# Retention attention and a routed MLP on one core: score blocks computed in 64x64 quadrants instead of 128x128 blocks

## The chip, the cores and the metric

The kernel runs on one core of a Trainium2 chip. The metric is the device time of one execution in microseconds (us). Matrix products run on TensorE (PE; its weight loads are listed apart as PEld), elementwise work on VectorE (DVE) and ScalarE (ACT). The queues of SyncE (SP), ACT and GpSimd (POOL) issue the transfers.

## The reference

Only this much of it matters here. For each of 8 batches and 8 heads, with 576 tokens and 64 features per head:

```python
scores = scale * np.matmul(q, k.transpose(0, 1, 3, 2))
gamma = 1.0 - 2.0 ** (-5.0 - np.arange(H))
Dmat = np.where(rel >= 0, gamma ** rel, 0.0)       # rel = query position - key position
ret = scores * Dmat
attn = np.matmul(ret, v)
```

The result is laid out as 4608 tokens by 512 features and goes through a gate (8 experts, each token to one expert with room for 576) and the chosen expert's two matrix products with a ReLU between them. Everything is in float32. What bears on the change: a score counts only where the key is not later than the query.

## The kernel before, in words

The attention stage goes through 16 units `u`; a unit is a pair of heads in a pair of batches, so four sequences of 576 tokens. Each sequence is cut into four chunks of 128 tokens and a tail of 64. The 64 features of two heads fill the 128 partitions of a `q` or `k` tile (partitions 0 to 63 and 64 to 127, `half(0)` and `half(1)`), and the two batches lie side by side.

The powers of gamma are split off: the values `v` are scaled by ScalarE (`vscale`), the output by a table `ex` when it leaves the accumulator (`evict`). So inside a 128-token chunk only the causal mask remains. Per half unit `hf` (two chunks, two batches: four blocks of 128 keys by 128 queries for each of two heads) the steps are:

- `A(u, hf)`, line 566: the scores of the chunks with themselves, keys on the output's partitions, queries on its columns, into the accumulator tile `pA` (two banks, one buffer). Line 568: VectorE multiplies `pA` by the mask `m1` and writes `am`.
- `A2(u)`, line 577: the tail's scores, in 64x64 pieces; masked into `amt`.
- `across`, line 601: earlier chunks' running state `S` times the queries, into `pX` (one buffer). The pieces are 64 by 64 with 128 query columns (64 for the tail).
- `ST`, line 589: the update of the state, evicted by ScalarE (line 591).
- `within`, line 610: `am` times the values, added in `pX`. `within2`, line 617: the same for the tail.
- `evict`, line 630: VectorE scales `pX` into the tile `xT`.
- "fills": pieces of the gate (lines 643, 656, 658), of row transposes and stores (lines 667, 675), and of the routing (lines 151 to 233), hung at fixed places between the units.

`A` is called half a unit ahead: the order on TensorE is A of the next half, (A2), across, ST, within, ST, (within2, across of the tail), fills. Each engine executes its queue in the order in which the program is written; nothing is reordered by the kernel. The loads of unit `u + 2` are issued on SP at the start of unit `u` into three rotating buffers, so they wait until unit `u - 1` has been read.

After the last unit the routing search, then eight experts' products follow; that part is not touched.

Of the kernel before, what the change touches and what calls it, by code (L numbers as in the profile page):

```python
# [10 lines left out]
F32 = mybir.dt.float32  # L11
# [3 lines left out]
ALU = mybir.AluOpType  # L15
# [3 lines left out]
B, H, S, D = 8, 8, 576, 64  # L19
NP, HP, NB = 4, 4, 9  # L20
N, DM, E, FF = 4608, 512, 8, 1024
SLACK = 1.0

CST = HP * 18 + 128 + 64

def consts_np():
    h = np.arange(H); g = (1.0 - 2.0 ** (-5.0 - h)).astype(np.float64)
    p = np.arange(128)
    at = np.where(np.arange(NB) < 8, 128 * (np.arange(NB) // 2), 512)[None] + np.where(np.arange(NB) < 8, p[:, None], p[:, None] % 64)
    vs = g.reshape(HP, 1, 2)[None] ** -at[:, None, :, None].astype(np.float64)  # L30
    m1 = p[:, None] <= p[None, :]
    m2 = p[:, None] % 64 <= np.arange(64)[None, :]
    ex = 0.125 * g.reshape(HP, 2)[:, p // 64].T[:, :, None] ** np.arange(S)
    f = lambda a: np.ascontiguousarray(a, dtype=np.float32).reshape(128, -1)
    return np.concatenate([f(vs), f(m1), f(m2), f(ex)], axis=1)

def layout(q, k, v):

    def pairs(a):
        a = a.reshape(NP, 2, HP, 2, S, D).transpose(0, 2, 3, 1, 4, 5)  # L40
        m = a[..., :512, :].reshape(NP, HP, 2, 2, 4, 128, D).transpose(0, 1, 2, 4, 3, 5, 6).reshape(NP, HP, 2, 1024, D)
        t = a[..., 512:, :].reshape(NP, HP, 2, 128, D)
        return np.concatenate([m, t], axis=3)
    second = np.concatenate([np.arange(1024) // 128 % 2, np.arange(128) // 64])[None, None, None, :, None] == 1
    cross = lambda a: np.where(second, a[:, :, ::-1], a)
    T = lambda a: cross(pairs(a)).transpose(0, 1, 2, 4, 3).reshape(NP, HP, 128, 1152)
    N = lambda a: a.reshape(NP, HP, 2, NB, 128, D).transpose(0, 1, 4, 3, 2, 5)
    vn = N(pairs(v)).copy()
    vn[:, :, :, 8, 1] = np.roll(vn[:, :, :, 8, 1], 64, axis=2)
    qk = np.ascontiguousarray(np.stack([T(q), T(k)], axis=2))  # L50
    vk = np.ascontiguousarray(np.concatenate([vn.reshape(NP, HP, 128, NB * 128), N(pairs(k)).reshape(NP, HP, 128, NB * 128)[..., :1024]], axis=3))
    return qk, vk
# [445 lines left out]
def attention(tc, nc, P, qk, vk, cst_d, wg_d, rf, xd, Lg):  # L498
    cst = P['c'].tile([128, CST + HP*S], F32, name="cst", tag="xg")
    vs = cst[:, 0:HP*18].rearrange("p (h q) -> p h q", h=HP)  # L500
    m1, m2 = cst[:, CST-192:CST-64], cst[:, CST-64:CST]
    ex = cst[:, CST:].rearrange("p (h q) -> p h q", h=HP)
    wg = P['a'].tile([128, HP, 32], F32, name="wg")
    LD = {}
# [16 lines left out]
    def consts(hp):  # L521
        part(CST + S*hp, CST + S*hp + S)
    load(0, "kqvn", (512,))
    load(1, "kqvn", (512,))

    def fetch(order):
        for x in order.split():
            if x == "c":
                part(0, CST)
            elif x[0] == "h":  # L530
# [6 lines left out]
    PS, AM, PX, XT = {}, {}, {}, {}  # L537
    ident = P['ident']
    SI = {}
    half = lambda x: slice(64*x, 64*x + 64)  # L540
# [7 lines left out]
            nc.scalar.activation(x, x, AF.Copy, scale=vs[:, u % HP, 4*c+h:4*c+h+1])  # L548

    two = P['open']("pa")  # L550
    PS2 = P['ps'].tile([128, 4, 64], F32, name="pS", tag="r", bufs=1)

    def A(u, hf):

        if u == 16: return
        if hf == 0 and 2 <= u + 1 < 16:
            if u < 3:
                consts(u + 1)
            if u == 2:
                R.fetch(nc, rf)  # L560
                nc.sync.dma_start(wg[:, :, 0:8], wg_d.rearrange("(hp p) e -> p hp e", p=128))
        pa = two.tile([128, 2, 4, 128], F32, name="pA", tag="A", bufs=1)
        for j in range(4):
            s = slice(512*hf + 128*j, 512*hf + 128*j + 128)
            for r in range(2):
                nc.tensor.matmul(pa[:, r, j], LD[u, 'k'][half(r), s], LD[u, 'q'][half(r), s], start=True, stop=True, skip_group_check=True)  # L566
        AM[u, hf] = P['w'].tile([128, 2, 4, 128], F32, name="am", bufs=2)
        nc.vector.tensor_tensor(AM[u, hf], pa, m1[:, None, None, :].to_broadcast([128, 2, 4, 128]), op=ALU.mult)  # L568

    def A2(u):  # L570

# [9 lines left out]
    def ST(u, c):  # L581

        if u == 16: return
        if c == 0: PS[u] = PS2[:, 2*(u % 2):2*(u % 2)+2]
        v, n = LD[u, 'v'], LD[u, 'n']
# [165 lines left out]
    vscale(0, 1)  # L751
    P['warm'](7)
    A(0, 0)
    ST(0, 0)
    nc.gpsimd.memset(wg, 0.0)
# [58 lines left out]
    c = R.first_digits(30, 36)  # L814
# [245 lines left out]
def build(tc, nc, qk, vk, cst, wg, rf, w1, w2, out):  # L1060
    with ExitStack() as top:
# [4 lines left out]
        top.enter_context(tc.manual_schedule())  # L1066
        xd = dr.tile([N, DM], F32, name="xd")
        full = P['c'].tile([128, 512], BF16, name="full")
# [66 lines left out]
```

## Time and profile before

| what | value |
|---|---|
| time, median of 3 runs | 650.63 us (650.55 to 651.21) |
| the profiled execution | 651.56 us, span 649.8 us |
| PE busy over the span | 610.9 us (94%) |
| VectorE busy over the span | 406.5 us (63%) |
| transfers of 576 KB of keys, issue to landing, median | 7.2 us |
| last masking of scores (line 568) starts | 136.8 us |

The attention stage fills the first 143 us or so of the span, the routing and the experts the rest. Busy shares count an engine as busy from the start of an instruction to its end; several matrix products can be under way at once, so a sum of their durations says less than the distance between their starts.

### The profile page before, as it was taken

The numbers are of one execution on the slowest core, as the hardware profiler recorded it, in microseconds if no ns is written. First come the engines' busy times: TensorE is split into PE (matmuls) and PEld (weight loads), VectorE is DVE, ScalarE is ACT, GpSimd is POOL, SyncE is SP. The second block draws the span as 40 slices with busy tenths as digits, with TensorE's granted clock in tenths as the row PEclk, the third lists the DMA queues.
The fourth block names the chain that finished last, engine by engine and source line by source line (L and its number), as shares of the span: only waits on it lengthen the run. The fifth ranks groups of instructions, "written<-read, shape, count | busy, mean of one in ns | idle before, by whom it ended". The sixth has DMA issues, their size and how long they took to land.

```text
span 649.8 us, 14770 instructions
## 1 busy us (share of the span) xinstructions
PE 610.9 (94%) x5756; PEld 519.3 (80%) x5756; DVE 406.5 (63%) x1504; ACT 288.8 (44%) x584; POOL 140.9 (22%) x189
## 2 busy tenths in 40 slices
PE   8899898978969998999999999988999999999995
PEld 5687777756569878977987898788779889989984
DVE  3567979778747887987996897777783302301300
ACT  4455555523265236552563356144615724643500
POOL 0000000000311072162153142241314234131111
PEclk9999999989979999999999999998999999999998
DMA  9998999743497469889599199747966995893521
GB/s 333 400 391 281 348 350 351 266 98 131 155 215 176 140 173 246 212 193 263 110 245 261 59 223 227 208 106 172 201 188 146 227 264 141 174 269 117 98 66 40
DMA packets 51704, 134.20 MB, mean 207 GB/s; under 512 B 5810, under 2 KB 19762, under 8 KB 51634
## 3 DMA queue, kind: packets, MB, share of 16 engines
q0 software_dynamic: 14960, 51.91, 36.7%
q1 hardware_dynamic: 36530, 81.08, 36.0%
q8 instruction: 45, 0.74, 0.5%
q10 hardware_dynamic: 144, 0.26, 0.1%
q14 instruction: 25, 0.20, 0.1%
HBM read 81.33 MB, written 18.87 MB: 154 GB/s over the span
## 4 chain that ended last, share of the span: by engine, by line
PE 68%; DVE 15%; DMA 6%; issue 6%; POOL 2%; ACT 2%; SPq 0%; POOLq 0%; DVEq 0%; ACTq 0%
PE ph L963 25%; PE py L1002 24%; PE pA L566 4%; PE pX L610 3%; DMA qin<-in_qk 2%; PE pS L589 2%; PE pX L601 2%; PE r L332 2%; PE pt L934 2%; DMA w1l<-raw 1%; PE pT L643 1%; DVE am L568 1%; DVE xT L630 1%; POOL xg L919 1%; DMA cst<-in_cst 1%
## 5 line engine op out<-in xcount | busy, mean ns | idle before, releaser
L1002 PE MATMUL py<-w2h,hb 128*128 128x512 f32 x576 | 188.2, 399 | 0.0
L963 PE MATMUL ph<-xh,w1h 128*128 128x320 f32 (+1 forms) x512 | 153.7, 304 | 2.7 <-ACT xh L936 1.5
L963 PE MATMUL ph<-xh,w1l 128*128 128x320 f32 (+1 forms) x512 | 151.3, 299 | 4.6 <-DMA w1l<-raw 4.2
L963 PE MATMUL ph<-xl,w1h 128*128 128x320 f32 (+1 forms) x512 | 151.0, 299 | 0.2 <-issue 0.2
L1002 PE MATMUL py<-w2l,hb 128*128 128x512 f32 (+1 forms) x320 | 125.1, 391 | 0.0
L1002 PEld LDWEIGHTS py<-w2h,hb 128*128 128x128 f32 x576 | 104.0, 188 | 20.6
L963 PEld LDWEIGHTS ph<-xh,w1l 128*128 128x128 f32 x512 | 97.7, 192 | 5.4 <-DMA w1l<-raw 4.4
L967 ACT ACTIVATE hb<-ph 128x256 fp32r<-128x256 f32 (+1 forms) x128 | 51.7, 410 | 112.5 <-PE ph L963 103.9
L963 PEld LDWEIGHTS ph<-xh,w1h 128*128 128x128 f32 x512 | 97.8, 192 | 4.7 <-ACT xh L936 1.9
L963 PEld LDWEIGHTS ph<-xl,w1h 128*128 128x128 f32 x512 | 97.9, 192 | 0.7 <-DVE cs L336 0.3
L970 DVE SCALAR_TENSOR_TENSOR hb<-ph,hb 128x256 fp32r<-128x256 f32 (+1 forms) x192 | 59.0, 352 | 60.2 <-ACT hb L967 56.6
L919 POOL DMA_INDIRECT xg<-xd,idx x40 | 40.8, 1020 | 202.1 <-DMA raw<-in_w 168.8
L1002 PEld LDWEIGHTS py<-w2l,hb 128*128 128x128 f32 (+1 forms) x320 | 56.7, 177 | 12.7
L979 POOL DMA_INDIRECT out_y<-yt,idx x40 | 40.9, 1022 | 118.4 <-ACT yt L1019 76.4
L1019 ACT ACTIVATE yt<-py 128x512 f32<-128x512 f32 x32 | 19.2, 598 | 105.3 <-PE py L1002 79.8
L908 POOL DMA_DIRECT2D w2l<-raw x32 | 28.8, 900 | 126.5 <-ACT hb L967 117.8
L548 ACT ACTIVATE vin<-vin,cst 128x128 f32<-128x128 f32 (+1 forms) x160 | 48.2, 379 | 6.8 <-DMA vin<-in_vk 6.8
L568 DVE TENSOR_TENSOR am<-pA,cst 128x1024 f32<-128x1024 f32 x32 | 39.1, 1221 | 18.0 <-PE pA L566 17.7
L1022 DVE TENSOR_TENSOR yt<-yt,py 64x512 f32<-64x512 f32 x8 | 5.4, 679 | 69.5 <-ACT yt L1021 69.3
L566 PEld LDWEIGHTS pA<-qin,kin 64*128 64x128 f32 x512 | 32.1, 191 | 16.1 <-DVE am L568 7.8
L566 PE MATMUL pA<-qin,kin 64*128 64x128 f32 x512 | 38.3, 289 | 6.9 <-DVE am L568 5.0
L591 ACT ACTIVATE S<-pS 128x128 f32<-128x128 f32 x64 | 17.6, 276 | 51.1 <-PE pS L589 51.1
(177 smaller groups left out, 877.4 us busy)
## 6 DMA issues: line engine op xcount, KB each, us to landing
raw<-in_w SPq DMA_DIRECT2D x64, 512.0 KB, 5.5
w2l<-raw POOLq DMA_DIRECT2D x32, 512.0 KB
w1l<-raw POOLq DMA_DIRECT2D x31, 512.0 KB
kin<-in_qk SPq DMA_DIRECT2D x14, 576.0 KB, 7.2
qin<-in_qk SPq DMA_DIRECT2D x14, 576.0 KB
vin<-in_vk SPq DMA_DIRECT2D x14, 576.0 KB, 7.2
nin<-in_vk SPq DMA_DIRECT2D x14, 512.0 KB, 10.5
xd<-xr SPq DMA_DIRECT2D x36, 192.0 KB, 4.0
```

What stands on the lines that cost most here:

```text
L548: nc.scalar.activation(x, x, AF.Copy, scale=vs[:, u % HP, 4*c+h:4*c+h+1])
L566: nc.tensor.matmul(pa[:, r, j], LD[u, 'k'][half(r), s], LD[u, 'q'][half(r), s], start=True, stop=True, skip_group_check=True)
L568: nc.vector.tensor_tensor(AM[u, hf], pa, m1[:, None, None, :].to_broadcast([128, 2, 4, 128]), op=ALU.mult)
L610: nc.tensor.matmul(PX[u, hf][half(h), b, 128*c:128*c+128], v[:, a:a+64], AM[u, hf][:, h ^ b, j], start=False, stop=False, skip_group_check ...
L908: nc.gpsimd.dma_start(lo, raw, accum_op=ALU.add)
L919: nc.gpsimd.indirect_dma_start(out=xg[:n, j, :], out_offset=None, in_=xd[:, :], in_offset=bass.IndirectOffsetOnAxis(ap=found[e][:n, j:j+1] ...
L963: T.matmul(ps, w, x, start=(k == 0), stop=(k == 11))
L967: A.activation(hb[:, f, c], ps, AF.Relu)
L970: V.scalar_tensor_tensor(hb[:, f, to+a:to+b], ps[:, a:b], 0.0, hb[:, f, 256*s+a:256*s+b].bitcast(F32), op0=ALU.max, op1=ALU.subtract)
L979: st = nc.gpsimd.indirect_dma_start(out=out[:, :], out_offset=bass.IndirectOffsetOnAxis(ap=found[e][:n, t:t+1], axis=0), in_=y[:n], in_off ...
L1002: T.matmul(ps[:m], a, w, start=(k == 0), stop=(k == last), skip_group_check=True)
L1019: A.activation(y, ps, AF.Copy)
```

## The change

The block of 128 keys by 128 queries is cut at key 64. The first 64 keys meet all 128 queries; the last 64 keys meet only the last 64 queries, since the mask leaves nothing of the first 64. Each piece is a product of its own with 64 keys on the output's partitions, so a block that was one product of 128 by 128 is now one of 64 by 128 and one of 64 by 64.

In every second chunk the keys (with their copies of `k` by row and their `v`) are turned by 64 tokens on the host, so that there the long piece lies on the other half of the output's partitions. The mask for these chunks is turned too: `m1` becomes a tile of two masks, copied twice side by side by VectorE at the start, and the constants grow by 128 columns (64 KB). `pA` becomes one tile for the whole stage, set to zero once at the start; the quarter that is never written stays zero, and the mask multiplies it by zero.

```diff
-    m1 = p[:, None] <= p[None, :]
+    m1 = np.stack([turned(c)[:, None] <= p[None, :] for c in range(2)], axis=1)
...
     two = P['open']("pa")
+    pa = two.tile([128, 2, 4, 128], F32, name="pA", tag="A", bufs=1)
+    nc.vector.memset(pa, 0.0)
+    nc.vector.tensor_copy(m1, cst[:, CST-320:CST-64].rearrange("p (c q) -> p c q", c=2)[:, :, None, :].to_broadcast([128, 2, 2, 128]))
...
-        pa = two.tile([128, 2, 4, 128], F32, name="pA", tag="A", bufs=1)
-        for j in range(4):
-            s = slice(512*hf + 128*j, 512*hf + 128*j + 128)
-            for r in range(2):
-                nc.tensor.matmul(pa[:, r, j], LD[u, 'k'][half(r), s], LD[u, 'q'][half(r), s], start=True, stop=True, skip_group_check=True)
+        k, q = LD[u, 'k'], LD[u, 'q']
+        for j in (0, 2, 1, 3):
+            s = 512*hf + 128*j
+            for t in (j//2, 1 - j//2):
+                x = 64*(t ^ j//2)
+                for r in range(2):
+                    nc.tensor.matmul(pa[half(t), r, j, x:], k[half(r), s+x:s+x+64], q[half(r), s+x:s+128], start=True, stop=True, skip_group_check=True)
         AM[u, hf] = P['w'].tile([128, 2, 4, 128], F32, name="am", bufs=2)
-        nc.vector.tensor_tensor(AM[u, hf], pa, m1[:, None, None, :].to_broadcast([128, 2, 4, 128]), op=ALU.mult)
+        nc.vector.tensor_tensor(AM[u, hf], pa, m1.rearrange("p c b q -> p (c b) q")[:, None].to_broadcast([128, 2, 4, 128]), op=ALU.mult)
```

On TensorE one half unit reads, before (unit 1's second step; a row is a run of equal products, with the output's shape):

```order
L566 MATMUL pA_212<-qin_92,kin_91 128x128 x8
L601 MATMUL pX_223<-qin_88,S_190 64x128 x4
L601 MATMUL pX_223<-qin_88,S_204 64x128 x4
L589 MATMUL pS_117<-vin_89,nin_90 64x64 x4
L610 MATMUL pX_223<-am_172,vin_89 64x128 x8
```

and in the changed kernel, where the same lines are 577, 612, 600 and 621:

```order
L577 MATMUL pA_118<-qin_93,kin_92 64x128 x2
L577 MATMUL pA_118<-qin_93,kin_92 64x64 x2
...
L577 MATMUL pA_118<-qin_93,kin_92 64x128 x2
L577 MATMUL pA_118<-qin_93,kin_92 64x64 x2
L612 MATMUL pX_248<-qin_89,S_208 64x128 x4
L612 MATMUL pX_248<-qin_89,S_222 64x128 x4
L600 MATMUL pS_121<-vin_90,nin_91 64x64 x4
L621 MATMUL pX_248<-am_190,vin_90 64x128 x8
```

Nothing changed places; the eight products of the block became sixteen (the pair of rows four times), and the other steps stand as they stood.

On VectorE the program begins, before, so (with the semaphores that a row waits for):

```order
L1069 MEMSET full_66 128x512
L1073 TENSOR_SCALAR ident_70<-it_68 128x128 [waits Pool_49]
L568 TENSOR_TENSOR am_139<-pA_130,cst_85 128x1024 [waits DMAHW2_49,PE_49]
```

and in the changed kernel so:

```order
L1080 MEMSET full_66 128x512
L1084 TENSOR_SCALAR ident_70<-it_68 128x128 [waits Pool_49]
L558 MEMSET pA_118 128x1024
L559 COPY m1_86<-cst_85 128x512 [waits DMAHW2_49]
L579 TENSOR_TENSOR am_150<-pA_118,m1_86 128x1024 [waits DVE_49,PE_49]
```

Two instructions came in ahead of the first masking, and the wait for the constants' transfer moved from the masking to the copy.

## Rows read from the trace of the kernel before

**Rows 1.** The page: busy time by engine, then the span in 40 slices (16.2 us each; tenths busy, the granted TensorE clock in tenths, the DMA engines' busy tenths).

```profile
PE 610.9 (94%) x5756; PEld 519.3 (80%) x5756; DVE 406.5 (63%) x1504; ACT 288.8 (44%) x584; POOL 140.9 (22%) x189
PE   8899898978969998999999999988999999999995
DVE  3567979778747887987996897777783302301300
PEclk9999999989979999999999999998999999999998
DMA  9998999743497469889599199747966995893521
```

**Rows 2.** The chain of work that ended last, in order of time: start, us, what it ran through. First the loading phase, then two bursts of line 566, the second six bursts (three units) after the first.

```profile
6.58 6.35 DMA cst<-in_cst
12.94 8.89 DMA qin<-in_qk
21.97 1.16 PE pA L566 x16
...
45.32 1.09 PE pA L566 x16
```

**Rows 3.** The shares of the span that this chain spends on each line, largest first (the row ends where the view cuts it).

```profile
by line: PE ph L963 24.8%; PE py L1002 24.0%; issue 6.0%; PE pA L566 3.6%; PE pX L610 3.1%; DMA qin<-in_qk 2.0%; PE pS L589 1.9%; PE pX L601 1.9%; PE r L332 1.7%; PE pt L934 1.6%; DMA w1l<-raw 1.4%; PE pT L643 1.3%; DVE am L568 1.2%; DVE xT
```

**Rows 4.** The timeline between 104 and 109 us, PE and two rows of DVE: start, us from the first start to the last end, engine, line, out<-in, partitions, shape, records; in brackets the idle time before.

```profile
104.25 1.16 PE L566 MATMUL pA<-qin,kin 64*128 64x128 f32 x16 [0.90 <-DVE am L568]
105.34 0.67 PE L601 MATMUL pX<-qin,S 64*64 64x128 f32 x16
105.94 0.45 PE L589 MATMUL pS<-vin,nin 128*64 128x64 f32 x8
106.22 1.05 PE L610 MATMUL pX<-am,vin 128*64 128x128 f32 x16
106.24 1.22 DVE L568 TENSOR_TENSOR am<-pA,cst 128x1024 f32<-128x1024 f32 x1
107.09 0.40 PE L589 MATMUL pS<-vin,nin 128*64 128x64 f32 x8
107.42 0.34 PE L617 MATMUL pX<-amt,vin 64*64 64x64 f32 x8
107.59 0.30 PE L601 MATMUL pX<-qin,S 64*64 64x64 f32 x8
107.82 1.16 PE L566 MATMUL pA<-qin,kin 64*128 64x128 f32 x16
107.95 0.89 DVE L630 TENSOR_TENSOR xT<-pX,cst 128x512 f32<-128x512 f32 x2 [0.50 <-PE pX L601]
108.91 0.39 PE L577 MATMUL pAt<-qin,kin 64*64 64x64 f32 x6
109.08 0.33 PE L601 MATMUL pX<-qin,S 64*64 64x128 f32 x2
```

**Rows 5.** Groups of instructions by line between 22 and 143 us, shapes apart: busy us, mean ns of one, idle before them and what ended it.

```profile
L568 DVE TENSOR_TENSOR am<-pA,cst 128x1024 f32<-128x1024 f32 x28 | 34.2, 1221 | 9.4 <-PE pA L566 9.2
L566 PE MATMUL pA<-qin,kin 64*128 64x128 f32 x448 | 32.7, 285 | 6.4 <-DVE am L568 5.0 <-DMA qin<-in_qk 1.2
L601 PE MATMUL pX<-qin,S 64*64 64x128 f32 x352 | 17.2, 282 | 2.5 <-DVE xT L630 1.7 <-issue 0.8
L630 DVE TENSOR_TENSOR xT<-pX,cst 128x512 f32<-128x512 f32 x28 | 19.3, 688 | 17.8 <-PE pX L601 13.5 <-PE pX L610 4.3
```

**Rows 6.** The page's list of DMA queues (packets, MB, share of 16 engines) and of transfers (KB each, median us from issue to landing).

```profile
q1 hardware_dynamic: 36530, 81.08, 36.0%
q8 instruction: 45, 0.74, 0.5%
...
kin<-in_qk SPq DMA_DIRECT2D x14, 576.0 KB, 7.2
```

**Rows 7.** Five stretches of the stage: length, then busy us and number of records of PE and PEld, of DVE, ACT and POOL; granted clock, DMA share, GB/s.

```profile
18.74:28.13 9.39, 6.67 (x126) 5.49 (x126) 4.17 (x6) 5.20 (x20) 0.00 (x0) 1.00 1.02 406
28.13:41.00 12.87, 12.36 (x254) 10.76 (x253) 7.88 (x36) 6.49 (x24) 0.00 (x0) 1.00 1.04 400
41.00:88.53 47.53, 45.50 (x886) 36.80 (x888) 37.67 (x76) 24.78 (x86) 0.00 (x0) 1.00 0.96 336
88.53:109.08 20.55, 18.56 (x390) 15.60 (x383) 17.17 (x40) 10.00 (x36) 0.00 (x0) 1.00 1.00 335
109.08:115.70 6.62, 6.40 (x134) 4.96 (x132) 4.77 (x8) 3.21 (x11) 0.00 (x0) 1.00 1.02 353
```

**Rows 8.** The timeline around three stops of PE, in the columns of rows 4; "issue" is a wait for nothing that the profile shows.

```profile
26.93 0.38 PE L601 MATMUL pX<-qin,S 64*64 64x128 f32 x2
28.14 0.44 PE L601 MATMUL pX<-qin,S 64*64 64x128 f32 x6 [0.83 <-issue]
...
41.01 0.34 PE L601 MATMUL pX<-qin,S 64*64 64x64 f32 x8 [0.42 <-issue]
...
115.22 0.29 PE L601 MATMUL pX<-qin,S 64*64 64x64 f32 x6
115.74 0.32 PE L601 MATMUL pX<-qin,S 64*64 64x64 f32 x2 [0.23 <-issue]
```

**Rows 9.** The queue "q8 instruction" alone, packets, MB and share, in five stretches, in this order: 18.7 to 41 us, 41 to 115.7 us, 25.6 to 26.8 us, 89.2 to 90.3 us, 113.5 to 114.6 us.

```profile
q8 instruction: 3, 0.05, 0.9%
q8 instruction: 11, 0.18, 0.9%
q8 instruction: 1, 0.02, 5.6%
q8 instruction: 1, 0.02, 5.8%
q8 instruction: 1, 0.02, 5.4%
```

**Rows 10.** The timeline of the start, in the columns of rows 4.

```profile
0.94 0.48 DVE L1069 MEMSET full<- 128x512 bf16 x1 [0.94 <-PEq L1125]
4.79 1.79 PEld L566 LDWEIGHTS pA<-qin,kin 64*128 64x128 f32 x16 [1.05 <-DMA qin<-in_qk]
6.92 1.22 DVE L568 TENSOR_TENSOR am<-pA,cst 128x1024 f32<-128x1024 f32 x1 [5.41 <-PE pA L566]
```

More of the change, by code (lines that the diff above doesn't have):

```diff
@@ L22 @@
 SLACK = 1.0
-CST = HP * 18 + 128 + 64
+CST = HP * 18 + 256 + 64
 def consts_np():
@@ L28, in consts_np @@
     p = np.arange(128)
-    at = np.where(np.arange(NB) < 8, 128 * (np.arange(NB) // 2), 512)[None] + np.where(np.arange(NB) < 8, p[:, None], p[:, None] % 64)
+    turned = lambda c: (p + 64 * (c % 2)) % 128
+    at = np.stack([128 * (b // 2) + turned(b // 2) if b < 8 else 512 + p % 64 for b in range(NB)], axis=1)
     vs = g.reshape(HP, 1, 2)[None] ** -at[:, None, :, None].astype(np.float64)
-    m1 = p[:, None] <= p[None, :]
+    m1 = np.stack([turned(c)[:, None] <= p[None, :] for c in range(2)], axis=1)
     m2 = p[:, None] % 64 <= np.arange(64)[None, :]
@@ L46, in layout, with N @@
     T = lambda a: cross(pairs(a)).transpose(0, 1, 2, 4, 3).reshape(NP, HP, 128, 1152)
-    N = lambda a: a.reshape(NP, HP, 2, NB, 128, D).transpose(0, 1, 4, 3, 2, 5)
-    vn = N(pairs(v)).copy()
+    def N(a):
+        a = a.reshape(NP, HP, 2, NB, 128, D).transpose(0, 1, 4, 3, 2, 5).copy()
+        odd = np.arange(8) // 2 % 2 == 1
+        a[:, :, :, :8][:, :, :, odd] = np.roll(a[:, :, :, :8][:, :, :, odd], 64, axis=2)
+        return a
+    vn = N(pairs(v))
     vn[:, :, :, 8, 1] = np.roll(vn[:, :, :, 8, 1], 64, axis=2)
@@ L500, in attention @@
     vs = cst[:, 0:HP*18].rearrange("p (h q) -> p h q", h=HP)
-    m1, m2 = cst[:, CST-192:CST-64], cst[:, CST-64:CST]
+    m2 = cst[:, CST-64:CST]
+    m1 = P['a'].tile([128, 2, 2, 128], F32, name="m1")
     ex = cst[:, CST:].rearrange("p (h q) -> p h q", h=HP)
```

## The prediction

> **What bounds the kernel now.** I read the page first: PE is busy nearly everywhere and at full clock in the attention stage, while the transfer engines are at nine tenths or more over most of the first eight slices [rows 1]. The chain says which of the two counts when: until 21.97 us it runs through transfers, afterwards through PE burst by burst [rows 2]. The changed line, 566, takes 3.6% of the span on that chain, 23.4 us, which at 1.09 us from a burst's start to the next step [rows 4] is some 21 bursts [rows 3]; 28 run between 22 and 143 us [rows 5]. So the scores bound this stage on PE, and from 143 us on nothing is touched: what the stage gains or loses should pass to the end unchanged.
>
> Two things stand close behind. VectorE: the eviction after a unit's tail starts at 107.95 and lasts 0.89 us, and the next step into the same accumulator starts at 109.08, hardly 0.2 us after it [rows 4]. And a queue that no line of the program names. "q8 instruction" moves 45 packets of 0.74 MB together [rows 6], 16 KB each. PE and PEld have 5756 records each [rows 1], and 11512 / 45 = 256: a packet looks like a block of 256 PE instructions of 64 bytes. The stretches bear that out: 252, 507, 1774, 773 and 266 records of PE and PEld [rows 7], or one, two, seven, three and one block within 4%, and three packets up to 41 us, eleven from there to 115.7 [rows 9]. Just at three of these borders PE stops for "issue": it goes on at 28.14, 41.01 and 115.74 [rows 8]. The packet had started after 25.6 us for the first stop and after 113.5 for the last [rows 9], so PE goes on up to 2.5 and 2.2 us after a packet's start, about 2.4. In other words, PE now and then waits for its own instructions, and these come over the same engines as the loads.
>
> **The change part by part.**
>
> *The bursts.* A product leaves two matrix and two load records (448 matrix records for 28 bursts of eight products [rows 5]). The trace already has pieces of the new kind: line 601's sixteen 64x128 records last 0.67 us in all, one of them 0.28 [rows 4, 5], so fifteen steps take 0.39 us: 0.026 us each, 0.104 for four quadrants side by side. For 64 columns I take a little over half, 0.06: the sixteen short records from 107.42 run out at 107.89 [rows 4], which less the length of one (some 0.22) makes 0.017 each, 0.067 for four. Each quadrant gets two long and two short products, two records each: 4 x 0.104 + 4 x 0.06 = 0.66 us. What follows a burst is again 64x64 work, so the 0.2 us between the last start (1.16 - 0.28 = 0.88) and the next step at 1.09 [rows 4] mostly go. New step about 0.69 instead of 1.09: 0.40 us saved. Bounds: 0.45, and below zero if the quadrants do not run side by side (a rival).
>
> Not all of it arrives. In a unit's first half the new burst would end at 108.49 and the tail's scores 0.18 later (108.91 to 109.08), but `pX` comes free only at 108.85: 0.2 of the 0.4 remain there. The mean of the two halves is 0.30, and 21 bursts give 6.3 us; if every burst kept only 0.2, 4.2.
>
> *The instructions.* A burst goes from 32 records (loads included) to 64, a unit from 72 products to 88, or 288 records to 352 without the fills. A block then holds 0.73 unit instead of 0.89.
>
> Early, the packets set the pace already: from 18.74 to 41.00 us there are three blocks, with stops at 28.14 and 41.01 [rows 7, 8]. If the packets come when they come now, PE has done 3 x 0.16 = 0.49 unit less at 41 us. Three units take 45.32 - 21.97 = 23.35 us [rows 2], one 7.8, so that is 3.8 us. I take 3.0, since the border is reached, and the next packet asked for, a little sooner; bounds 0 and 3.8. The five bursts before 41 us then save nothing: 1.5 of the 6.3 is struck off.
>
> Later, 41 to 115.7 us: eleven blocks in 74.7 us, 6.8 us each. With some 19 bursts more by 32 records it would be 13.4 blocks in 69 us, 5.15 each. A packet is in time if it starts within 5.15 - 2.4 = 2.75 us of PE's entry into the block before (4.4 us now). The entry at 88.53 had its packet at 89.2, after 0.7 us; the entry at 109.08 at 113.5, after 4.4, behind the loads [rows 7, 9]. A 576 KB load needs 7.2 us to land [rows 6], so waits between 0.7 and 4.4 are what a packet meets. Spread evenly, 45% exceed 2.75, by 0.83 on the mean: 0.37 us per block, 5.9 us over some 16 blocks until the loads end (the DMA row falls in the eighth slice, 114 to 130 us [rows 1]). I take half, 3.0: while PE stops, VectorE catches up, and PE's waits for it (5.0 and 1.7 us, rows of line 566 and 601 [rows 5]) shrink. Bounds 0 and 5.9.
>
> *The start.* Setting `pA` to zero: no row has this size; the 512-column one takes 0.48 us [rows 10], so 0.5 to 1.2. It ends by about 2.7 us and the first burst waits for `qin` until 4.79. The mask's copy of 512 columns, 0.3 to 0.7 us, lies in the 5.41 us for which VectorE waits before 6.92 [rows 10]. Without that cover either would cost its length once. The 64 KB more of constants go down a stream of some 400 GB/s [rows 7] which the start waits for: 0.2 us. Masking has the same 1024 columns [rows 5]: 1.22 us as before, 0 for the second mask's layout.
>
> **Sum:** -(6.3 - 1.5) + 3.0 + 3.0 + 0.2 = +1.4 us. The profiled execution took 651.56 us (span 649.8), 0.9 above the median; I apply the difference to the median of 650.63: 652.0.
>
> **The rivals.**
>
> *The saving comes through.* If the packets ask earlier because PE goes faster and lie hidden, the terms of 3.0 go: -6.3 + 0.2 = -6.1, 644.5 us; with one or two microseconds of stops, 646. For it: of eleven borders after 41 us only the one at 115.74 shows a stop. Against: three borders stop already, and the blocks come a quarter faster. The Trainium skill's "Runtime: NRT & Kernel Launch", section "Instruction fetch mechanics", speaks for this rival: instructions come in blocks of 256 (16 KiB), and the price of crossing into a new one is said to be mostly hidden. The trace agrees on the 256; on "hidden" it disagrees at 28.14 us. By that rule the sum would be the -6.1.
>
> *The loads bound.* DMA share is 0.96 to 1.04 from 18.74 us on [rows 7]; a faster PE then asks sooner and gets nothing sooner. Against: after 22 us line 566 waits for `qin` only 1.2 us [rows 5]. Between 41.00 and 88.53 us 4% is free, 1.9 us. At most that much is won, some 1.2: 649.4.
>
> *The quadrants run one column half after the other.* A burst would be 2 x 0.66 = 1.32 us, 0.23 longer than now: 21 x 0.23 = 4.8 us, and with the early 3.0 it is 658.4. It decides once a burst's step is over 1.09. Against: line 601's four quadrants overlap [rows 4], and neighbouring products of the new order lie in different quadrants.
>
> **How the numbers follow.** Something under 0.2% (1.3 us) can't be told from no change in this kernel. Forecast, packets eat the saving: chance 0.56, 652.0, own range 649 to 655. Saving comes through: 0.24, 644.5 to 648. Loads bound: 0.12, 649.4. No overlap: 0.08, 658.4. All bounds of the sum together run from 644.5 to 650.63 - (4.2 - 1.0) + 3.8 + 5.9 + 0.2 = 657.3; leaving out about one in ten at each end, 646.5 to 655.5. Faster (under 649.3): the 0.24 and 0.03 of the forecast's lower edge, 0.27. Same (649.3 to 651.9): the loads' 0.12 and 0.16 of the forecast, 0.28. Slower: 0.37 of it and the 0.08, 0.45.
>
> **What would show it.** The burst's step: 0.65 to 0.75 us from line 577's first start to the next line's. The packets: 48 to 50 of them instead of 45 (28 bursts plus four, 32 records more each, are four blocks), and PE stops for "issue" at borders of 256 records, more than 4 us of them before 45 us and some of 0.3 to 1 us later. The first burst still starts at about 4.8 us, masking still takes 1.22 us. The last masking, at 136.8 us now, at 138. I am wrong if the stops between 22 and 130 us together stay under 3 us (then it is faster), if packets start sooner after the entry than now, or if the step is over 1 us.

## The result: 0.5 to 0.6% slower, and the profile after

| | changed | before, same chip | ratio (95% interval) |
|---|---|---|---|
| first chip | 653.46 us | 649.23 us | 1.0058 (1.0034 to 1.0082) |
| again, another chip | 648.98 us | 645.26 us | 1.0046 (1.0018 to 1.0075) |

The times are medians of all runs; the ratios leave out one of the 20 and one of the 12 runs of the changed kernel, which fell into a slower state. By the ratios the change costs 3 to 4 us (the medians lie 4.2 and 3.7 us apart); 1.4 were forecast, with slower as the likeliest sign. The absolute times of before differ by several us from chip to chip, so only ratios on one chip are compared below. The profiled execution of the changed kernel has a span of 652.8 us. From its page, in the columns of [rows 1] and [rows 6]:

```profile
PE 600.9 (92%) x6264; PEld 512.0 (78%) x6268; DVE 407.4 (62%) x1506; ACT 288.5 (44%) x584; POOL 141.0 (22%) x189
PE   7889888977877999999999999989999999999995
PEclk8989999989997999999999999999999999999999
q8 instruction: 49, 0.80, 0.5%
```

PE has 508 records more and PEld 512, and PE is busy for 10 us less; it waits more in the first slices. The mean granted clock of the execution is the same (0.985, before 0.986), but the first and the third slice show an 8 where before has a 9; the third is followed up below. The q8 queue moves 49 packets instead of 45: the 16 KB blocks of 256 instructions are confirmed by number. Where the 10 us went stands in the groups by line between 22 and 143 us (columns of [rows 5]; 577, 612 and 641 are the former 566, 601 and 630, and 579, which masks, the former 568):

```profile
L577 PE MATMUL pA<-qin,kin 64*64 64x128 f32 x437 | 25.2, 276 | 8.7 <-DVE am L579 6.2 <-issue 2.4
L577 PE MATMUL pA<-qin,kin 64*64 64x64 f32 x436 | 24.0, 223 | 0.1
L612 PE MATMUL pX<-qin,S 64*64 64x128 f32 x352 | 17.3, 281 | 4.6 <-DVE xT L641 2.7 <-issue 1.9
```

and in the list of PE's waits in the same stretch (line waited for: us in total, times, longest):

```profile
PE pA L577 <- DVE am L579: 6.2, 6, 1.5
PE pX L612 <- issue: 3.0, 3, 1.5
PE pX L612 <- DVE xT L641: 2.7, 4, 2.1
PE pA L577 <- issue: 2.4, 1, 2.4
PE pS L600 <- issue: 2.1, 3, 0.8
PE pX L621 <- issue: 0.4, 1, 0.4
PE pAt L588 <- issue: 0.3, 1, 0.3
```

The rows with "issue" add up to 8.2 us in nine stops, at five different lines: a stop belongs to no operation, it comes where a block of 256 instructions ends. Counted over everything in PE's own queue (matrix products, weight loads and 109 others, semaphores above all), the nine stops lie whole multiples of 256 instructions apart, without an exception. The same list of the kernel before has 1.5 us in three stops. The waits for VectorE grew by 1.2 (`am`) and 1.0 us (`xT`).

Two bursts from the timeline around the place of [rows 4]:

```profile
106.16 0.90 PE L577 MATMUL pA<-qin,kin 64*64 64x128 f32 x32 [0.54 <-DVE am L579]
106.22 0.68 DVE L641 TENSOR_TENSOR xT<-pX,cst 128x512 f32<-128x512 f32 x1
106.96 0.67 PE L612 MATMUL pX<-qin,S 64*64 64x128 f32 x16
...
101.71 0.90 PE L577 MATMUL pA<-qin,kin 64*64 64x128 f32 x32 [1.40 <-DVE am L579]
102.42 0.39 PE L588 MATMUL pAt<-qin,kin 64*64 64x64 f32 x7
```

The burst at 101.71 is followed after 0.71 us; most are (0.72, where no stop falls into them). The burst at 106.16 takes 0.80: the eviction of `pX` ends at 106.90 and line 612 needs `pX`. That happens four times between 22 and 143 us.

And one stop followed to its packet: two stretches between borders (columns of [rows 7]), then the queues from 86.4 to 90.0 and from 90.1 to 91.2 us, then PE at the border (the row before it and the row behind it).

```profile
86.37:92.60 6.23, 5.12 (x127) 4.50 (x127) 2.85 (x5) 2.32 (x9) 0.00 (x0) 1.00 0.98 354
92.60:97.77 5.17, 5.17 (x127) 3.90 (x127) 3.68 (x7) 3.37 (x13) 0.00 (x0) 1.00 0.98 279
...
q1 hardware_dynamic: 386, 1.50, 101.6%
...
q8 instruction: 1, 0.02, 5.9%
...
91.20 0.29 PE L612 MATMUL pX<-qin,S 64*64 64x64 f32 x6
92.60 0.27 PE L612 MATMUL pX<-qin,S 64*64 64x64 f32 x2 [1.12 <-issue]
```

PE enters a block at 86.37. For 3.6 us the loads alone fill the transfer engines (101.6%), and only then, after 90.1, the packet moves. It has landed by 91.2, and PE goes on at 92.60, 1.12 us after it ran dry. The 127 + 127 records of that block would have run in about 5.2 us, as those of the next one did; a packet that starts some 3.7 us after the entry and lets PE go on 2.5 us after its start needs 6.2.

One thing more stands in no list of waits. Before the change the granted clock is 1.00 from 22 to 139 us. In the changed kernel it is 0.50 (1.2 instead of 2.4 GHz) between 35.9 and 39.2 us, just behind the longest stop. Here are that stop, the next burst and the stretch between them, then the same two rows of the second chip's trace (e12_changed), where the clock is 1.00 at this place:

```profile
35.37 0.43 PE L577 MATMUL pA<-qin,kin 64*64 64x128 f32 x7 [2.40 <-issue]
39.25 0.90 PE L577 MATMUL pA<-qin,kin 64*64 64x128 f32 x32
35.90:39.20 3.30, 3.30 (x44) 2.90 (x40) 1.65 (x3) 0.28 (x1) 0.00 (x0) 0.50 1.03 412
...
36.12 0.43 PE L577 MATMUL pA<-qin,kin 64*64 64x128 f32 x7 [2.13 <-issue]
38.42 0.90 PE L577 MATMUL pA<-qin,kin 64*64 64x128 f32 x32
```

The same work takes 3.88 us at the lower clock and 2.30 us at full clock, 1.6 us more. Yet the block entered at 35.37 lasts 6.31 us in the one trace and 6.19 us in the other: the second chip's PE runs through sooner and then stops for 1.29 us at the next border, since its packet comes no sooner. So the lower clock stands here in the place of a stop, and the 8.2 us are too few by about that stop. The second chip's trace has its own stretch at 0.50, from 62.2 to 65.6 us, behind a stop of 2.07 us; from burst to burst it takes 4.82 us there and 3.41 in the first trace, 1.4 us more, and at its next border PE does not stop in either trace. Not every long stop is followed by such a stretch: e8_full has stops of up to 2.3 us and a granted clock of 1.00 throughout the stage. What decides it was not tested.

### The profile page after: what moved, and what is told of

Read it like the earlier page. It is cut to its first block, busy times and chain, and to the rows that moved or that the text cites. A ratio compares the mean times of both kernels' runs of the same rounds, so it can differ in the third digit from the quotient of the medians.

```text
span 652.8 us, 15792 instructions
## 1 busy us (share of the span) xinstructions
PE 600.9 (92%) x6264; PEld 512.0 (78%) x6268; DVE 407.4 (62%) x1506; ACT 288.5 (44%) x584; POOL 141.0 (22%) x189
## 4 chain that ended last, share of the span: by engine, by line
PE 66%; DVE 16%; issue 7%; DMA 6%; ACT 2%; POOL 1%; SPq 0%; POOLq 0%; DVEq 0%; ACTq 0%
PE ph L974 25%; PE py L1013 25%; PE pX L621 3%; PE pA L577 2%; PE pS L600 2%; DMA raw<-in_w 2%; PE pX L612 2%; PE r L337 2%; PE pt L945 2%; DVE am L579 1%; DVE xr L678 1%; DMA w1l<-raw 1%; DMA qin<-in_qk 1%; PE pT L654 1%; DVE G L168 1%
## 5 line engine op out<-in xcount | busy, mean ns | idle before, releaser
L579 DVE TENSOR_TENSOR am<-pA,m 128x1024 f32<-128x1024 f32 x32 | 39.0, 1218 | 13.1 <-PE pA L577 12.8
L641 DVE TENSOR_TENSOR xT<-pX,cst 128x512 f32<-128x512 f32 (+2 forms) x49 | 25.3, 544 | 26.0 <-PE pX L612 19.6
L577 PEld LDWEIGHTS pA<-qin,kin 64*64 64x64 f32 x1024 | 24.9, 137 | 20.5 <-DVE am L579 8.3
## 6 DMA issues: line engine op xcount, KB each, us to landing
nin<-in_vk SPq DMA_DIRECT2D x14, 512.0 KB, 10.6
```

Of the source, the lines that this page charges most:

```text
L577: nc.tensor.matmul(pa[half(t), r, j, x:], k[half(r), s+x:s+x+64], q[half(r), s+x:s+128], start=True, stop=True, skip_group_check=True)
L579: nc.vector.tensor_tensor(AM[u, hf], pa, m1.rearrange("p c b q -> p (c b) q")[:, None].to_broadcast([128, 2, 4, 128]), op=ALU.mult)
L641: nc.vector.tensor_tensor(dst, src, e, op=ALU.mult)
```

## The experiments

Two counts of stops occur. The expectations add up, at every border of 256 instructions between 22 and 142 us, the time from the last start of a PE or PEld record before it to the first start behind it (2.4 us before, 11.3 us in the changed kernel; the usual step from one record to the next, and waits for other engines that fall on a border, are in it). The table gives that count and the sum of the "issue" rows in the list of PE's waits between 22 and 143 us, which holds the stops alone. "Last masking" is the start of the last `am` of the stage. Both counts and the last masking come from one profiled execution of each kernel.

| kernel | ratio to before (95% interval) | gaps at borders, us | "issue" waits, us | last masking, us |
|---|---|---|---|---|
| before | 1 | 2.4 | 1.5 | 136.8 |
| changed, first and second chip | 1.0058, 1.0046 | 11.3, 10.6 | 8.2, 8.7 | 138.6, 139.6 |
| e1_halves | 1.0337 (1.0299 to 1.0375) | 1.4 | 0.5 | 158.5 |
| e2_after_light | 0.9947 (0.9920 to 0.9974) | 3.8 | 2.9 | 129.6 |
| e3_before_light | 0.9982 (0.9956 to 1.0008) | 0.7 | none | 134.6 |
| e4_lockstep | 1.0092 (1.0065 to 1.0118) | 10.3 | 7.8 | 139.8 |
| e5_long_only | 0.9930 (0.9898 to 0.9961) | 4.0 | 2.7 | 132.8 |
| e6_after_paced | 1.0117 (1.0073 to 1.0160) | 8.6 | 6.4 | 139.8 |
| e7_before_paced | 1.0035 (1.0007 to 1.0064) | 1.0 | 0.3 | 137.5 |
| e8_full | 1.0120 (1.0066 to 1.0174) | 14.4 | 11.5 | 142.8 |
| e9_late | 1.0003 (0.9976 to 1.0030) | 2.4 | 1.1 | 135.7 |
| e10_first | 1.0028 (1.0005 to 1.0050) | 7.2 | 5.4 | 137.2 |
| e11_second | 1.0051 (1.0026 to 1.0077) | 5.2 | 3.3 | 137.0 |

The theory: TensorE waits for its own instructions, because a longer program asks for packets faster than they get past the loads. Rivals: the quadrants or the new layout cost something themselves; the saving is only smaller than thought; the loads bound the stage.

### The longer code without the saving, first try: e1_halves

```diff
-            for r in range(2):
-                nc.tensor.matmul(pa[:, r, j], LD[u, 'k'][half(r), s], LD[u, 'q'][half(r), s], start=True, stop=True, skip_group_check=True)
+            for x in (0, 64):
+                for r in range(2):
+                    nc.tensor.matmul(pa[:, r, j, x:x+64], LD[u, 'k'][half(r), s], LD[u, 'q'][half(r), s.start+x:s.start+x+64], start=True, stop=True, skip_group_check=True)
```

> The kernel before with each 128x128 score block of a burst written as two 128x64 products: the same quadrants, the same query columns in all, but 64 PE records in a burst instead of 32, which is what the changed kernel has. Theory (the longer code makes TensorE stop): the program has 352 records in a unit instead of 288, the q8 queue moves 48 to 50 packets instead of 45, TensorE stops at many of the borders of 256 records after 22 us for 7 to 11 us in all as in the changed kernel, against 3 us before; the burst step stays at 1.05 to 1.15 us, so nothing is saved, and the kernel is 5 to 12 us slower than before (655 to 662 us), slower than the changed kernel. Rival (the shorter products themselves, or the rotated keys, are what costs): the columns and the layout are those of before, the stops stay near 3 us, and the time is within 2 us of before.

Measured: 3.4% slower, and both theories missed, because the burst did not stay at 1.1 us (timeline):

```profile
101.94 2.00 PE L567 MATMUL pA<-qin,kin 64*128 64x64 f32 x32
103.87 0.34 PE L602 MATMUL pX<-qin,S 64*64 64x128 f32 x4
```

The step went from 1.09 to 1.93 us with the same query columns in all. What doubled is the number of products, each with its load of 64x128 weights; so the pace goes by the products on such weights and not by the columns. Whether it is the load itself or a fixed price of such a product, this run can't tell. With such slow bursts the blocks last longer (6.5 us on the mean between 41 and 115 us) and hardly a stop is left, as the theory wants, but as a test of the code alone this run is void. e8_full took its place.

### The longer code with the whole block: e8_full

```diff
-                    nc.tensor.matmul(pa[half(t), r, j, x:], k[half(r), s+x:s+x+64], q[half(r), s+x:s+128], start=True, stop=True, skip_group_check=True)
+                    nc.tensor.matmul(pa[half(t), r, j], k[half(r), s+x:s+x+64], q[half(r), s:s+128], start=True, stop=True, skip_group_check=True)
```

> The changed kernel with the short products as long as the others: 64 keys with all 128 queries of the chunk, so that the whole block is computed again as in the kernel before, but in sixteen products of a burst instead of eight (64 PE records, quadrants, turned keys). This is the longer code without the saving. Theory (code is the price): the burst step is 1.04 to 1.10 us as before if a burst goes by columns per quadrant; 49 packets; stops between 22 and 142 us of 4 to 11 us, a little less than in the changed kernel as the blocks take longer to run; the time is 4 to 10 us over the kernel before and 0 to 5 us over the changed kernel. Rival (code costs nothing, the saving is just smaller than forecast): the time is within 2 us of the kernel before. For the burst step: if 0.80 us in the changed kernel was set by the number of records or by the weights, the step stays at 0.80 to 0.90 us.

```profile
103.87 1.10 PE L577 MATMUL pA<-qin,kin 64*64 64x128 f32 x32 [1.30 <-DVE am L579]
104.79 0.35 PE L588 MATMUL pAt<-qin,kin 64*64 64x64 f32 x6
...
PE pX L612 <- issue: 3.7, 3, 2.3
PE pS L600 <- issue: 3.6, 4, 1.3
PE pA L577 <- issue: 3.0, 2, 2.0
```

The time came as the theory said: 1.2% slower, although a burst is shorter than before. The burst step did not come as it said: 0.92 us, neither the 1.04 to 1.10 of the columns nor the 0.80 to 0.90 of the number of records. So the same 512 query columns in each quadrant, with weights of 64 columns instead of 128, run 0.17 us faster than the block in one piece. Of the 0.37 us that the change saves in a burst, 0.17 come from cutting and only 0.20 from the quarter left out. The stops are more than in the changed kernel (14.4 us against 11.3 and 10.6 at the borders), not less, and above the 4 to 11 us expected. Blocks last longer here (6.05 us on the mean between 41 and 115 us, 5.75 in the changed kernel), so their length alone does not foretell the stops; why the packets come later here (3.41 us after the entry on the mean, against 3.15) stays open.

### The loads made lighter: e2_after_light and e3_before_light

```diff
         for i in what:
+            if u >= 2 and i in "kn":
+                LD[u, i] = LD[u % 2, i]
+                continue
```

> The changed kernel without the loads of k and n from unit 2 on (units 2 to 15 use k and n of units 0 and 1; the loads are what is left out of the computation). About half of the loaded bytes are gone, and TensorE's work and code are those of the changed kernel. Theory (the code packets of TensorE start late because they wait behind the loads on the same DMA engines): packets on q8 start sooner after a border is passed (under 1.5 us instead of 1.3 to 4.1 us), the stops of TensorE at the borders after 22 us shrink from about 9 us to under 4 us, and the time falls to 640 to 648 us; against the kernel before with the same loads left out it is 3 to 6 us faster, so the sign of the change turns. Rival (the stops have nothing to do with the loads, only with the length of the code): stops of 7 us or more remain, and the difference to the kernel before with the same loads left out stays at +3 to +5 us.

> The kernel before without the loads of k and n from unit 2 on (units 2 to 15 use k and n of units 0 and 1; the loads are what is left out of the computation), the partner of the changed kernel with the same loads left out. Theory (code packets wait behind the loads): before had only some 3 us of stops, so it gains at most 3 us from them and 0 to 3 us from the first units' loads: 643 to 649 us, and it is 3 to 6 us slower than its partner. Rival (loads have nothing to do with it): the partner stays 3 to 5 us slower than this kernel.

Between 16 and 142 us the DMA share falls from 0.91 to 0.65 (the changed kernel, then its partner with the loads left out, then before with the loads left out; columns of [rows 7]):

```profile
16.00:142.00 126.00, 106.60 (x2712) 87.20 (x2706) 94.71 (x214) 61.31 (x215) 0.00 (x0) 0.98 0.91 317
16.00:142.00 126.00, 110.84 (x2810) 89.93 (x2811) 101.87 (x252) 65.02 (x223) 0.00 (x0) 1.00 0.65 201
16.00:142.00 126.00, 118.81 (x2341) 96.94 (x2345) 97.25 (x218) 62.52 (x219) 0.00 (x0) 0.99 0.64 197
```

Measured: 643.99 us with the change and 647.81 without, on one chip: the change now wins 3.8 us by the medians and 3.1 by the means, where with all loads it costs 3 to 4. The last maskings start at:

```profile
129.57 1.22 DVE L582 TENSOR_TENSOR am<-pA,m 128x1024 f32<-128x1024 f32 x1
...
134.56 1.22 DVE L571 TENSOR_TENSOR am<-pA,cst 128x1024 f32<-128x1024 f32 x1
```

5.0 us apart in favour of the change; the two profiled executions are the shortest of the one kernel (640.64 us) and the longest of the other (650.38), so the times compare better than these two traces. The lower clock of the changed kernel (0.98 in the first of the three rows) is gone with the stops (1.00). Its stops shrink to 2.9 us, all of them before 41 us save a trace (0.1 us of gaps at borders behind 41 us, 7.0 in the changed kernel). Packets of blocks entered between 41 and 115 us start 1.61 us after the entry on the mean (under 1.5 was expected), against 3.15 in the changed kernel. The code is the same, the bursts are the same; so the sign of this change hangs on whether the packets stand behind loads. The rival "only the length of the code" falls. The kernel before gains little from lighter loads: its stage ends 2.3 us sooner, and its time can't be told from no change (the interval holds 1). So the loads' own landing is not what bounds it.

### Only the long products: e5_long_only

```diff
-        for j in (0, 2, 1, 3):
-            s = 512*hf + 128*j
-            for t in (j//2, 1 - j//2):
-                x = 64*(t ^ j//2)
+        for js, x in (((0, 2), 0), ((1, 3), 0)):
+            for j in js:
+                s, t = 512*hf + 128*j, x//64 ^ j//2
```

> The changed kernel without the short (64x64) products of the score bursts: the scores of the later 64 keys of a chunk with its later 64 queries are what is left out of the computation. A burst has 32 PE records again, as before, and all else (quadrants, turned keys, pA as one tile, two masks) is as in the changed kernel. Theory (the extra 32 records are the price): 45 or 46 packets on q8, the stops at borders of 256 records between 22 and 142 us fall back to 1 to 4 us in all (before 2.4, changed kernel 11.3), and the time is 4 to 9 us under the kernel before. If the burst's 0.80 us goes by columns, its step is some 0.5 to 0.55 us here. Rival (the quadrants, the single pA tile or the turned layout is the price): stops or waits of the changed kernel's size remain and the time is at or above that of the kernel before.

```profile
104.98 0.67 PE L576 MATMUL pA<-qin,kin 64*64 64x128 f32 x16
105.47 0.41 PE L587 MATMUL pAt<-qin,kin 64*64 64x64 f32 x8
...
q8 instruction: 45, 0.74, 0.5%
```

45 packets, 2.7 us of stops, 0.7% faster with all loads in place: quadrants, layout, the single `pA` and its masks cost nothing that shows; so it is the 32 records more in a burst that do. The step of 0.49 us saves 0.60 in each of 28 bursts, 16.8 us, and the stage ends just 4.0 us sooner: behind PE stands VectorE (waits for `am` 8.2 us instead of 5.0, for `xT` 2.8 instead of 1.7), and the granted clock is 0.96 between 16 and 142 us instead of 0.99. These do not add up to the whole difference.

### The order inside a burst: e4_lockstep

```diff
-        for j in (0, 2, 1, 3):
-            s = 512*hf + 128*j
-            for t in (j//2, 1 - j//2):
-                x = 64*(t ^ j//2)
+        for js, x in (((0, 2), 0), ((0, 2), 64), ((1, 3), 0), ((1, 3), 64)):
+            for j in js:
+                s, t = 512*hf + 128*j, x//64 ^ j//2
```

> The changed kernel with the order of the products in a burst changed, so that the four quadrants of TensorE run products of the same length side by side (two long ones of 128 columns, two short ones of 64, twice); the number of records and of columns is the same. Theory (the burst takes 0.80 us instead of the 0.69 us forecast because long and short products beside each other end together only at the longer one): the burst step falls to 0.65 to 0.72 us. As the stops for code set the pace after 22 us, little of these 0.1 us x 21 shows: the time is 0 to 2 us under the changed kernel (651.5 to 653.5 us). Rival (0.80 us is what 64 records cost to issue, whatever their order): the burst step stays at 0.78 to 0.82 us and the time does not change. Rival (the burst's length is what decides, not the code): the time falls by the full 2 us or more, to 651 us or under, with a burst step of 0.70 us.

```profile
105.82 0.90 PE L576 MATMUL pA<-qin,kin 64*64 64x128 f32 x32 [1.09 <-DVE am L578]
106.61 0.67 PE L611 MATMUL pX<-qin,S 64*64 64x128 f32 x16
```

The step is the same to 0.01 us, 0.72 in most bursts and 0.80 in this one, as at the same place of the changed kernel. I had taken 0.80 as the rule, from bursts that wait for `pX`; as far as the step shows, no product waits for a longer neighbour. The order is indifferent, and the time shows no gain.

### The loads in two groups: e6_after_paced and e7_before_paced

```diff
-            load(u + 2, "kqvn")
+            load(u + 2, "kq")
+        if blk == 4 and u + 2 < 16:
+            pace = P['w'].tile([1, 1], F32, name="pace", bufs=2)
+            nc.sync.dma_start(pace, AM[u, 1][0:1, 0, 0, 0:1])
+            load(u + 2, "vn")
```

> The changed kernel with the loads of a unit split in two groups: q and k of unit u + 2 are issued where all four were, v and n later, behind a transfer of 4 bytes that waits for the unit's second masking. Nothing is left out. The same bytes move, in backlogs half as long. Theory (an instruction packet waits for the loads that are queued ahead of it): the packets start sooner after a border (mean under 2.7 us between 22 and 142 us against 3.3 in the changed kernel), the stops there fall from 11.3 us to 4 to 8 us, and the time falls by 2 to 6 us against the changed kernel, to 645 to 650 us beside 647 to 649 for the kernel before. Rival (only the amount moved counts, not the backlog, or v and n now come too late): stops unchanged or PE waits for vin or nin, and the time is that of the changed kernel or longer.

> The kernel before with its loads split in the same two groups, v and n of a unit behind a transfer of 4 bytes that waits for the second masking. Theory: before has only 2.4 us of stops for instructions between 22 and 142 us, so there is little to win: 0 to 2 us under the kernel before, and less than the changed kernel wins by the same edit. Rival (splitting the loads helps by something else than instructions): it gains as much as the changed kernel does, 2 us or more.

Both missed in time. In e6_after_paced the stops shrank only to 6.4 us (8.6 at the borders, 4 to 8 expected), and the waits for `am` took their place (9.3 us instead of 6.2):

```profile
PE pA L577 <- DVE am L579: 9.3, 9, 1.8
PE pA L577 <- issue: 2.9, 2, 2.1
```

The packets of blocks entered between 41 and 115 us start a little sooner, 2.66 us after the entry on the mean against 3.15 in the changed kernel. Both paced kernels are slower than before (e7_before_paced by 0.35%, where 0 to 2 us faster was expected), and no faster than without pacing. One reason can be read from SP's waits in the changed kernel: its queue already stands 25.9 us for `pX` (line 612), so its loads go out as buffers come free, and there may have been no backlog of four to halve; that is argued, not shown. Whether finer pieces or another queue would let packets through sooner was not tried.

### Half the dose: e9_late, e10_first, e11_second, with the changed kernel beside them

In these three a condition selects whole blocks in eight products (`u < 13`, `hf == 1`, `hf == 0`). The host turns `v` and the copy of `k` by row, but not the tile `kin`; it is the order of the pieces that turns the scores. So in the whole blocks of a second chunk the keys lie unturned, and the turned mask and values meet other scores there; the work is the same.

```diff
+        if hf == 1:
+            for j in range(4):
+                s = slice(512*hf + 128*j, 512*hf + 128*j + 128)
+                for r in range(2):
+                    nc.tensor.matmul(pa[:, r, j], k[half(r), s], q[half(r), s], start=True, stop=True, skip_group_check=True)
-        for j in (0, 2, 1, 3):
+        for j in () if hf == 1 else (0, 2, 1, 3):
```

> The changed kernel, but units 0 to 12 compute their bursts as whole 128x128 blocks in eight products again; only units 13 to 15 (six bursts) use the quadrants. Turned keys, the single pA tile and two masks stay. Theory (the saving of 0.37 us a burst is real and is eaten by stops for instructions only while loads run): the loads end soon after unit 13 begins, so six bursts save some 2 us with at most 1 us of new stops; 46 packets on q8, stops of 1.5 to 4 us between 22 and 142 us, and the time is 0.5 to 2.5 us under the kernel before (ratio 0.996 to 0.999). Rival (layout, mask or pA as one tile cost something of their own): 1 us or more over the kernel before.

> The changed kernel with the quadrants only in the bursts of each unit's first half (hf = 0); the other half's bursts are whole blocks in eight products. A unit has 320 PE records, half way between 288 and 352. Theory (a block of 256 records must last longer than a packet's wait of up to 4 us, its transfer of 1.0 us and 1.4 us until TensorE goes on): blocks of 256 records take some 6.2 us without stops, against 6.8 in the kernel before and 5.2 in the changed one, so the stops between 22 and 142 us come out between their 2.4 and 11.3 us, at 4 to 8 us, against 5 us saved by 14 bursts: 0 to 4 us over the kernel before. Rival (stops come only with blocks much shorter than 6 us): stops stay under 3 us and the time is 2 to 4 us under the kernel before.

> The changed kernel with the quadrants only in the bursts of each unit's second half (hf = 1); the bursts of the first half are whole blocks in eight products. As with the first half, a unit has 320 PE records. Theory: stops between 22 and 142 us of 4 to 8 us, 0 to 4 us over the kernel before. Rival (stops come only with much shorter blocks): under 3 us of stops, 2 to 4 us under the kernel before. The two halves differ by less than 2 us, unless the wait of the next step for pX (in the profile of the changed kernel four bursts step 0.80 us instead of 0.72 because of it) decides which half's saving arrives.

> The changed kernel itself once more, on the same chip as the three mixed kernels, so that they can be compared with it directly. Expected: 2 to 6 us over the kernel before (ratio 1.003 to 1.009), stops for instructions of 9 to 13 us between 22 and 142 us; the mixed kernels lie between the two by the theory.

With 320 records a unit, the stops are 5.4 and 3.3 us, between the 1.5 and 8.2 to 8.7 of the ends, and the medians lie 1.8 and 3.0 us over before, with the changed kernel's 3.7 beside them; by the ratios (1.0028 and 1.0051, beside 1.0046) the times can't be told from the changed kernel's, so the order shows in the stops alone. A block of 256 records lasts 6.2 to 6.3 us there (mean between 41 and 115 us), with 6.8 before and 5.75 in the changed kernel, and the stops grow as it is shortened by more instructions (e1_halves, at 6.5 us, has hardly one). Which half keeps the quadrants makes no difference that the intervals can tell. e9_late has as few stops as before and masks for the last time 1.1 us sooner, half of the 2 us expected, but no gain shows in the time (0.9976 to 1.0030). None of the kernels that do all the work beats before.

## Why the prediction was right, point by point

- **Sign and size.** Forecast +1.4 us, measured +4.2 and +3.7: the sign is right, the size is not. The time of 653.46 us lies inside the range of 649 to 655 and near the forecast of 652.0, but part of that is luck: the forecast stood on three runs of before at 650.63, and the median of 20 is 649.23. Taken from its own base the range is -1.6 to +4.4, and +4.2 is close to its upper end. At the last masking the forecast was 138; it starts at 138.6 and, on the other chip, 139.6:

```profile
138.57 1.22 DVE L579 TENSOR_TENSOR am<-pA,m 128x1024 f32<-128x1024 f32 x1
```

  So 1.75 to 2.8 us of the loss lie in the stage. The remaining 1 to 2.5 us are not located: from the last masking to the span's end it is 513.0 us before, 514.2 after, and 506 to 515 in the other runs, and that spread hides them.
- **The burst's step.** Forecast 0.69, within 0.65 to 0.75; measured 0.72, and 0.80 in the four bursts that wait for `pX`, a wait that the forecast had named. The split of this saving was not seen: I priced the new burst by its columns and never asked what 64x128 weights cost the old one (e1_halves, e8_full).
- **What arrives of it.** With 6.7 us more of "issue" waits between 10 and 143 us (9.0 against 2.3) and a stage 1.75 us longer, 4.95 us of the saving arrived as the rest; the forecast had 4.8. On the second chip it is 6.4 - 2.8 = 3.6 (its stage is compared with the one trace of before, on another chip).
- **The clock.** The forecast has no term for it: it read PE at full clock before the change and took that over. The stretches at 0.50 took 1.6 us on the first chip, in the place of a stop of about 1.3, and 1.4 us on the second. Counted beside the stops, some 6.5 and 5.0 us of the saving arrived, more than forecast, and the lower clock took part of it back. So that 4.95 falls so near to 4.8 is luck.
- **The stops, early.** Forecast +3.0 up to 41 us. The "issue" waits from 10 to 41.2 us are 4.3 us instead of 1.7: +2.6. (+1.7 on the second chip.)
- **The stops, later.** This is the term of the sum that was most mis-sized: forecast +3.0, measured 4.7 against 0.6 us, so +4.1, and +4.7 on the second chip; single stops reached 1.5 us, and 2.1 on the second chip, where 0.3 to 1 was given. The step in it that failed is halving the evenly spread 5.9 us because VectorE catches up. VectorE did not catch up: PE's waits for it rose from 6.7 to 8.9 us. Nor do the packets' starts spread as evenly as taken: they come 3.15 us after the entry on the mean (blocks entered between 41 and 115 us), later than before's 2.27; why later was not settled.
- **The packets.** 49, within 48 to 50, and all nine stops between 22 and 143 us at a border of 256 instructions. The Trainium skill's "Runtime: NRT & Kernel Launch", section "Instruction fetch mechanics", calls the crossing mostly hidden. With the loads cut that agrees with the trace (no "issue" wait at all in e3_before_light between 22 and 143 us); with the loads in place and 352 records a unit it does not (8.2 us).
- **The start.** As forecast: zeroing `pA` takes 0.91 us (0.5 to 1.2 was given) and lies in front of the first burst at 4.77; the copy of the mask takes 0.43 us.

```profile
1.72 0.91 DVE L558 MEMSET pA<- 128x1024 f32 x1 [0.21 <-issue]
4.77 1.01 PE L577 MATMUL pA<-qin,kin 64*64 64x128 f32 x32
5.12 0.43 DVE L559 COPY m<-cst 128x512 f32<-128x512 f32 x1 [2.49 <-DMA cst<-in_cst]
```

- **The rivals.** "The saving comes through" is what happens without half of the loads, with 3 to 4 us of its 6.1 (e2_after_light against e3_before_light). "The loads bound" falls with e5_long_only, which is faster with all loads. "One column half after the other" falls with the step of 0.72.

## What to carry to other kernels

Count instructions as a cost where a stage is bound by TensorE and full of loads: find the instruction queue's packets, divide PE's and PEld's records by them, and compare the time of one block with the longest wait of a packet behind the loads plus the 2.2 to 2.6 us from its start until TensorE goes on. A change that makes the work shorter by more and smaller products moves that limit the wrong way, and the stops it buys stand under no line of the program, only as "issue" at changing places. Before leaving out masked columns, ask whether columns or weights set the pace of the products: here nearly half of the saving of a burst came from cutting the products to narrower weights, with no column left out.

## What had not been expected of the hardware

- Products on 64x128 weights set the pace of the float32 score blocks, not their columns: 16 matrix records on such weights step in 1.09 us, 32 with half the columns each in 1.93 (e1_halves), and 32 on weights of 64x64 with all columns in 0.92 (e8_full). On 64x64 weights columns count again: a quarter less of them gives 0.72.
- The granted clock fell to 0.50 for a stretch in each trace of the changed kernel, behind a stop of 2.1 to 2.4 us, and the work in it took 1.4 to 1.6 us longer, which no list of waits shows; once this took the place of a stop for a packet, once it did not.
- However late a packet came, TensorE went on no sooner than 1.2 us after it had landed, in all the stops of all these runs.
- Taking away half of the loads halved the packets' waits (3.15 to 1.61 us on the mean); moving half of them to a later point shortened them to 2.66 at best, and no gain in time came of it.
